# Decays by a tree of pairs, and another order of the groups of an RWKV-7 attention kernel with hash-routed experts

## The chip, the cores and the metric

The kernel runs on one core of one Trainium2 chip. Its time is the device time of the execution in microseconds (us); lower is better. A core has five engines that run side by side, each through its own list of instructions in order: TensorE (PE, matrix products and transposes into PSUM), VectorE (DVE), ScalarE (ACT), GpSimd (POOL) and SyncE (SP, which here only issues DMA). In this kernel the order on PE, DVE, ACT and POOL is fixed by the program itself; SP's is chosen by the framework.

## The reference, cut to what matters

Two layers, one behind the other. The first is a recurrence over 768 steps for 4 batches x 8 heads with a 40 x 40 state:

```python
for t in range(S):                                     # S = 768, D = 40
    y[:, :, t] = einsum('bhd,bhde->bhe', r_t, state)
    Sa = einsum('bhde,bhe->bhd', state, a_t)
    state = state * w_t[:, :, None, :] - einsum('bhd,bhe->bhde', Sa, b_t) + einsum('bhd,bhe->bhde', v_t, k_t)
```

Its output, turned to 3072 rows of 320, goes to 8 experts, chosen by a hash of the token's id:

```python
expert_idx = token_ids * 2654435761 % 8
out[mask_e] = np.maximum(x[mask_e] @ w1[e], 0) @ w2[e]     # 320 -> 1024 -> 320
```

## The kernel before: the parts that matter

The recurrence is done in chunks of 64 steps. A *tile* is one chunk of two batches; there are 24 (tile `u`). Four tiles make a *group*, and two chunks of all batches make a *round of decays* (6 rounds; round `ri` serves tiles 4ri to 4ri+3). Within a chunk the products of `w` scale the other inputs: `pb` holds the reciprocals of such products, `qb` the products up to the chunk's end. Each group needs the inverse of triangular matrices, done by substitution on DVE.

Every piece of work is put down with a *tick*; the program sorts them by tick and writes them out in that order. Within a tick the position is given by a name:

```python
STEPS = ["r1", "r0", "z", "nc", "y", "at_t", "x", "x_t", "s", "u", "r_t", "sd", "a", "rc"]
LAG = 8          # tile u is recurred on (tile_b) at tick u + 8; its inputs are prepared (tile_a) at tick u
GRP = 4
```

The round of decays, in segments of 8 steps:

```python
def decays(ri, t_w, t0, span, t_f, span_f=None, stores=None):
    @at_tick(t_w)
    def _():
        x["qb"] = qb = early.tile([P, (HC + 1) * D], F32, tag="qb", name="qb", bufs=2)
        ...                                   # four DMAs load w into qb
        x["pb"] = early.tile([P, (HC + 1) * D], F32, tag="pb", name="pb", bufs=2)[:, 0:HC * D]
        nc.gpsimd.memset(segs(x["pb"])[:, :, 0, :], 1.0)

    for i in range(1, SL):                    # SL = 8: seven products of 128 x 160
            p = segs(x["pb"])
            nc.vector.tensor_tensor(p[:, :, i], p[:, :, i - 1], segs(x["qb"])[:, :, i - 1], op=OP.mult)
    for i in range(SL - 2, -1, -1):           # and seven more
            q = segs(x["qb"])
            nc.vector.tensor_tensor(q[:, :, i], q[:, :, i], q[:, :, i + 1], op=OP.mult)
    ...     # own: the products of the segments
    ...     # f_ps: PE brings the partner half's product; ends; rends = 1 / ends (128 x 160)
    ...     # half_p, half_q: pb * rends and qb * ends, two products of 128 x 640 each
    ...     # round 0: two transposes to p_rows, q_rows in SBUF; else: both are stored to DRAM
```

The preparation of a tile, and the inversion of a group:

```python
def tile_a(u):
    @at_tick(u - 1.7)      # loads: pl, ql (the decays, by GpSimd), al, kb (a, b, k, by SyncE); two buffers each
    ...
    @at_tick({0: -0.6, 1: -0.4, 2: 0.4, 3: 1.4}.get(u, u + late - (0.1 if late else 0.6)))
        ...                # DVE: at = -a * p ; z = kb * q
    @at_tick(u + late, "at_t")   # PE turns at, ACT copies
    @at_tick(u + late, "z")      # PE turns z, ACT copies
    @at_tick(u + late, "a")      # PE: the scores a_ps; ACT copies pk, no; DVE: mk

def group_i(gi, t0, t1, t2):
    ...     # DVE: nu <- pk (a transpose), 30 pairs outer = u * n, u += outer, then ut, ug (two transposes)
```

The recurrence of a tile, where PE's order is what the change touches:

```python
def tile_b(u, t0):
    @at_tick(t0 - 1, "r0")      # r1_ps  = at_t x sb     (sb: the state, copied by ACT at "rc" of tile u - 2)
    @at_tick(t0, "r1")          # r1_ps += mk x v        ; ACT copies r1
    @at_tick(t0, "nc")          # um x r1                ; ACT copies into x
    @at_tick(t0, "x_t")         # PE turns x             ; ACT copies
    @at_tick(t0, "s")           # s_ps = state + z x x   ; DVE: st = s_ps * decay
    @at_tick(t0, "rc")          # rc_ps = r_t x x_t      ; DVE: mr
    @at_tick(t0 + 1, "y")       # y = r_t x sd + mr x z  ; DVE: xs = y * p ; GpSimd stores xs
    @at_tick(t0 + 1, "sd")      # PE turns the state     ; ACT copies
    # tile_m: "x" and "u" at t0 - 1 use ut, ug of the group's inverse; tile_s: loads r, v at t0 - 2
```

And where it all stands:

```python
decays(0, -4.0, -3.0, 0.4, -2.5, 0.3)
decays(1, -2.9, -1.9, 0.4, (-0.55, ...), stores=1.34)
decays(2, -0.65, 0.87, 0.45, (1.87, 1.9, ...), stores=3.34)
for ri in range(3, NR):
    t0 = ri * RN * NG - 5.0                  # ri * 4 - 5
    decays(ri, t0 - 1.0, t0 + 0.25, 1.0, t0 + 1.3, 1.1)
for gi in range(NU // GRP):
    t0 = gi * GRP + GRP - 1 + t_a
    group_i(gi, t0 + 0.05, t0 + 0.1, t0 + 3.4)
# routing(): which token goes to which slot of which expert, in small steps on DVE
    t = 4.5 if i < 1 else NU + 3.35 + 0.105 * (i - 12) if i > 11 else 9.3 + 1.1 * i
```

The expert layer follows after the last tile: matrix products over eight experts, whose weights stream in.

Of the kernel before, what the change touches and what calls it, by code (L numbers as in the profile page):

```python
# [36 lines left out]
F32 = mybir.dt.float32  # L37
# [10 lines left out]
def kernel(  # L48
# [90 lines left out]
    def early_weights():  # L139
# [3 lines left out]
        w2s[0] = [early.tile([P, (C // 2 + 1) * D], F32, tag=n, name=f"w2_0{n}", bufs=2)[:, 0:FP // 2 * DM]  # L143
# [24 lines left out]
    STEPS = ["r1", "r0", "z", "nc", "y", "at_t", "x", "x_t", "s", "u", "r_t", "sd", "a", "rc"]  # L168
# [143 lines left out]
    SEG = 4  # L312
    HC = C // 2
    SL = HC // SEG

    def decays(ri, t_w, t0, span, t_f, span_f=None, stores=None):
# [4 lines left out]
        def segs(t):  # L321
            return t[:, 0:HC * D].rearrange("p (s t e) -> p s t e", s=SEG, e=D)
# [12 lines left out]
        @at_tick(t_w)  # L335
        def _():
            x["qb"] = qb = early.tile([P, (HC + 1) * D], F32, tag="qb", name="qb", bufs=2)

            dma = (nc.sync.dma_start, nc.scalar.dma_start if ri < 2 else nc.sync.dma_start)
            for y in range(2 * RN):  # L340
                src = w.rearrange("b h (n t) e -> (b h) n (t e)", t=HC)[:, ri * 2 * RN + y]
                dma[y % 2](qb[y * BH:(y + 1) * BH, 0:HC * D], src)
            x["pb"] = early.tile([P, (HC + 1) * D], F32, tag="pb", name="pb", bufs=2)[:, 0:HC * D]
            nc.gpsimd.memset(segs(x["pb"])[:, :, 0, :], 1.0)


        for i in range(1, SL):
            @todo.append
            def _(i=i):
                p = segs(x["pb"])  # L350
                nc.vector.tensor_tensor(p[:, :, i], p[:, :, i - 1], segs(x["qb"])[:, :, i - 1], op=OP.mult)
        for i in range(SL - 2, -1, -1):
            @todo.append
            def _(i=i):
                q = segs(x["qb"])
                nc.vector.tensor_tensor(q[:, :, i], q[:, :, i], q[:, :, i + 1], op=OP.mult)

        @todo.append
        def _():

            q = segs(x["qb"])
            x["own"] = own = work.tile([P, SEG, D], F32, tag="own", name="own", bufs=1)
            nc.vector.tensor_copy(own[:, SEG - 1], q[:, SEG - 1, 0])
            for s in range(SEG - 2, -1, -1):
                after_s = q[:, s + 1, 0] if s == SEG - 2 else own[:, s + 1]
                nc.vector.tensor_tensor(own[:, s], q[:, s, 0], after_s, op=OP.mult)  # L366

        def half_p(some):

            p = segs(x["pb"])[:, some]  # L370
            by = x["rends"][:, some].unsqueeze(2).to_broadcast([P, SEG // 2, SL, D])
            nc.vector.tensor_tensor(p, p, by, op=OP.mult)

        def half_q(some):
            q = segs(x["qb"])[:, some]
            by = x["ends"][:, 1:][:, some].unsqueeze(2).to_broadcast([P, SEG // 2, SL, D])
            nc.vector.tensor_tensor(q, q, by, op=OP.mult)

        @then.append
        def _():  # L380
            x["f_ps"] = p = bank([P, D], "f_ps")
            nc.tensor.matmul(p, lhsT=partner[:], rhs=x["own"][:, 0], start=True, stop=True)  # L382

        @then.append
        def _():

            x["ends"] = ends = work.tile([P, SEG + 1, D], F32, tag="ends", name="ends", bufs=1)
            nc.vector.tensor_scalar(ends[:, SEG], x.pop("f_ps"), second[:, 0:1], None, op0=OP.add)
            nc.vector.tensor_tensor(ends[:, 0:SEG], x["own"][:],
                                    ends[:, SEG].unsqueeze(1).to_broadcast([P, SEG, D]), op=OP.mult)  # L390

        @then.append
        def _():
            ends = x["ends"]
# [867 lines left out]
```

## Time and profile before

| | |
|---|---|
| time, median of 3 runs | 668.7 us (665.96 to 676.79) |
| the profiled execution, span | 663.8 us |
| PE, DVE, ACT, POOL busy | 562.9, 365.7, 296.7, 195.3 us |
| attention part, about | 0 to 411 us |
| expert layer, about | 411 to 664 us |
| DMA packets | 195,771, of which 176,718 under 512 B |
| moved | 85.14 MB |

The profile is of one execution. Its page gives the busy time of each engine, the span in 40 slices with tenths of busy time, the DMA queues, a chain of work that ended last, groups of instructions by line, and DMA issues. Answers of the trace give the same for any stretch: tables of stages, instructions in order of time with the idle time before each and who ended it, and lists of who waited for whom. "L479" is line 479 of the kernel; a line can be that of a helper that many operations share, so the names of the tiles tell more. Idle time of an engine that holds nobody up costs nothing.

### The profile page before, as it was taken

How to read it: one execution, taken by the hardware profiler on the slowest of the kernel's cores; microseconds unless marked ns; L12 is line 12 of the kernel's file. 1: busy time of each engine (PE TensorE's matmuls, PEld its weight loads, DVE VectorE, ACT ScalarE, POOL GpSimd, SP SyncE). 2: the span in 40 equal slices, each digit the busy share in tenths (PEclk: the TensorE clock that was granted, in tenths of full speed). 3: DMA queues.
4: the chain of work that ended last, by engine and by line, in shares of the span. 5: the costliest groups of instructions: out<-in, count | busy, mean ns of one | idle time of the engine just before them, and what ended most of it. 6: DMA issues, size and time to landing. Idle time of an engine off the chain costs nothing.

```text
span 663.8 us, 23022 instructions
## 1 busy us (share of the span) xinstructions
PE 562.9 (85%) x9866; PEld 428.9 (65%) x9866; DVE 365.7 (55%) x944; ACT 296.7 (45%) x695; POOL 195.3 (29%) x333
## 2 busy tenths in 40 slices
PE   0145558988988899899999988999999999999995
PEld 0134557777777788788888877775665656565653
DVE  6996977977886798689589843132030302023020
ACT  4043535765666687777767664112241313111010
POOL 0413331333333435334223321173314131212101
PEclk9976558998988999999999999999999999999999
DMA  7699996888488569774334541859243354121000
GB/s 133 175 169 177 162 168 114 157 156 152 104 158 157 117 129 185 125 142 96 62 81 83 126 127 34 267 183 318 89 152 90 129 199 161 48 100 40 30 12 24
DMA packets 195771, 85.14 MB, mean 128 GB/s; under 512 B 176718, under 2 KB 186191, under 8 KB 195664
## 3 DMA queue, kind: packets, MB, share of 16 engines
q1 hardware_dynamic: 184208, 46.25, 36.3%
q0 software_dynamic: 11264, 36.72, 19.7%
q8 instruction: 78, 1.28, 0.8%
q10 hardware_dynamic: 192, 0.66, 0.4%
q14 instruction: 29, 0.24, 0.1%
HBM read 66.54 MB, written 15.40 MB: 123 GB/s over the span
## 4 chain that ended last, share of the span: by engine, by line
PE 47%; issue 22%; DVE 14%; ACT 6%; DMA 5%; POOL 4%; SPq 1%; POOLq 0%; DVEq 0%; ACTq 0%
PE up_ps L1005 6%; PE dn_ps L1023 6%; PE y_ps L289 5%; PE s_ps L289 4%; PE x_t_ps L690 3%; PE a_ps L289 3%; PE t_ps L530 3%; PE r_ps L289 2%; POOL out_dram L1028 2%; PE z_ps L493 2%; PE x_ps L289 2%; PE nc_ps L289 2%; PE u_ps L289 2%; DVE outer L572 2%; PE sd_ps L750 2%
## 5 line engine op out<-in xcount | busy, mean ns | idle before, releaser
L1013 DVE TENSOR_SCALAR ht<-up_ps 128x416 f32<-128x416 f32 (+2 forms) x36 | 19.4, 543 | 166.1 <-PE up_ps L1010 164.7
L1023 PE MATMUL dn_ps<-w,ht 128*128 128x320 f32 x336 | 91.7, 433 | 0.0
L1005 PE MATMUL up_ps<-xt,w 128*128 128x416 f32 x224 | 81.3, 516 | 0.0
L1023 PEld LDWEIGHTS dn_ps<-w,ht 128*128 128x128 f32 x336 | 63.3, 190 | 25.5
L742 POOL DMA_DIRECT2D x_rows<-xs x44 | 23.2, 533 | 179.8 <-DVE xs L738 79.0
L1028 POOL DMA_INDIRECT out_dram<-o,idx_all x26 | 26.1, 1004 | 169.8 <-ACT o L1027 163.4
L572 DVE TENSOR_TENSOR outer<-nu 128x252 f32<-128x252 f32 (+8 forms) x180 | 63.4, 352 | 4.6
L579 DVE TENSOR_TENSOR nu<-nu,outer 128x252 f32<-128x252 f32 (+8 forms) x180 | 63.3, 352 | 4.5
L1005 PEld LDWEIGHTS up_ps<-xt,w 128*128 128x128 f32 x224 | 41.9, 190 | 36.8 <-issue 31.7
L1015 ACT ACTIVATE ht<-up_ps 128x416 f32<-128x416 f32 (+2 forms) x36 | 17.2, 479 | 107.5 <-PE up_ps L1010 107.4
L495 ACT COPY z_t<-z_ps 104x512 f32<-104x512 f32 x48 | 25.7, 588 | 66.0 <-PE z_ps L493 66.0
L1027 ACT COPY o<-dn_ps 128x320 f32<-128x320 f32 x26 | 11.1, 425 | 92.5 <-PE dn_ps L1023 92.5
L493 PE MATMUL z_ps<-ident,z 128*104 128x128 f32 x192 | 33.3, 331 | 15.2 <-DVE z L479 14.7
L460 POOL DMA_DIRECT2D pl<-p_rows x48 | 25.2, 531 | 51.7 <-DVE at L475 34.1
L289 PE MATMUL a_ps<-at_t,z_t 64*64 64x64 f32 x1536 | 32.0, 241 | 6.9 <-ACT at_t L531 6.9
L493 PEld LDWEIGHTS z_ps<-ident,z 128*104 128x104 f32 x192 | 26.0, 157 | 18.0 <-issue 15.5
L289 PEld LDWEIGHTS a_ps<-at_t,z_t 64*64 64x64 f32 x1536 | 28.4, 152 | 12.5 <-ACT at_t L531 9.5
L289 PE MATMUL rc_ps<-r_t,x_t 64*64 64x64 f32 x1536 | 29.9, 222 | 7.4 <-issue 6.7
L702 DVE TENSOR_TENSOR mr<-rc_ps,after 128x1024 f32<-128x1024 f32 x24 | 29.2, 1217 | 12.3 <-PE rc_ps L289 12.2
L523 DVE TENSOR_TENSOR mk<-a_ps,after 128x512 f32<-128x512 f32 x24 | 16.5, 688 | 30.5 <-ACT no L521 30.5
L289 PEld LDWEIGHTS rc_ps<-r_t,x_t 64*64 64x64 f32 x1536 | 25.8, 134 | 9.6 <-issue 8.5
L382 PE MATMUL f_ps<-own,partner 128*128 128x40 f32 x12 | 3.2, 359 | 33.6 <-DVE own L366 33.6
(227 smaller groups left out, 1168.6 us busy)
## 6 DMA issues: line engine op xcount, KB each, us to landing
ql<-q_rows POOLq DMA_DIRECT2D x48, 160.0 KB, 4.6
w<-in_moe_w_dram SPq DMA_DIRECT2D x10, 640.0 KB, 8.7
w<-in_moe_w_dram SPq DMA_DIRECT2D x10, 512.0 KB, 3.7
al<-in_a_dram SPq DMA_DIRECT2D x48, 80.0 KB, 4.6
kb<-in_b_dram SPq DMA_DIRECT2D x48, 80.0 KB, 4.1
kb<-in_k_dram SPq DMA_DIRECT2D x48, 80.0 KB, 4.1
pl<-p_rows POOLq DMA_DIRECT2D x48, 80.0 KB, 4.1
r<-in_r_dram SPq DMA_DIRECT2D x48, 80.0 KB, 3.9
```

Of the source, the lines that this page charges most:

```text
L289: nc.tensor.matmul(out_, lhsT=lhsT, rhs=rhs, start=start, stop=stop, skip_group_check=True)
L460: nc.gpsimd.dma_start(pl[half(be)], of_batches(p_rows, 2 * g + be, 1))
L493: nc.tensor.transpose(p[0:R, be, hp * P:(hp + 1) * P], x["z"][:, be, hp, :], ident[:])
L495: nc.scalar.copy(t[0:R, be].rearrange("p h t -> p (h t)"), p[0:R, be])
L530: nc.tensor.transpose(p[:, hp, :], src[:, hp, :], ident[:])
L572: nc.vector.tensor_tensor(tv, paired(x["u"])[:, 0:full[1], j:j + 1, :].to_broadcast(full), paired(x["n"])[:, j // 2, j + 1:, j % 2].unsque ...
L579: nc.vector.tensor_tensor(o, o, x["t"][:, 0:n].rearrange("p (c i k) -> p c i k", c=full[1], k=2), op=OP.add)
L702: nc.vector.tensor_tensor(t[:].rearrange("p two h t -> p (two h) t"), p[:].rearrange("p two (h t) -> p (two h) t", t=C), after[:].unsqueez ...
L742: dma(x_of[2 * g + be, n * C:(n + 1) * C], xs[half(be), :])
L1005: nc.tensor.matmul(p[:], lhsT=w1[c][:, (f0 + i) * P:(f0 + i + 1) * P], rhs=xt[:, c, 0:n], start=(c == 0), stop=False)
L1023: nc.tensor.matmul(p[i * m:(i + 1) * m], lhsT=ht[:, f, c0:c0 + m], rhs=w2[f // (FP // 2)][:, f % (FP // 2), :], start=(f == 0), stop=(f == ...
L1028: st = nc.gpsimd.indirect_dma_start(out=out[:], out_offset=bass.IndirectOffsetOnAxis(ap=idx, axis=0), in_=o[0:m], in_offset=None, bounds_c ...
```

## The change

Five things are changed together.

- **The tree.** A round of decays makes its running products by a tree of pairs: up through five levels of products of neighbours (widths 320, 160, 80, 40, 40 per side), then down again (40, 80, 160, 320, 640). It does the same with fewer elements. `w` is loaded into a tile of its own, `wt`, with one buffer, and is read until the end of the way down.
- **The order of PE's groups.** `STEPS` has another order, and `r0` of a tile stands at its own tick, ahead of `r1`, not a tick earlier.
- **The third round of decays** (`decays(2, ...)`) moves from ticks 0.87 to 2.2 behind the first inversion, to 7.2 to 8.1, and the fourth to 8.6 to 10.4.
- **The third group of tiles** (8 to 11) is prepared at ticks 10.4 to 11.75, close together, tiles 12 and 13 at 12.5 and 13.2; the group's inversion follows.
- **The routing's** first steps move from ticks 10.4 to 21.4 to 24.05 to 27.05, and one of its tiles shares memory with another.

The purpose is to let the first inversion, which the recurrence waits for, begin without the third round's work and stores in front of it, and to take work off DVE.

```diff
-    STEPS = ["r1", "r0", "z", "nc", "y", "at_t", "x", "x_t", "s", "u", "r_t", "sd", "a", "rc"]
+    STEPS = ["r0", "r1", "z", "y", "nc", "x", "at_t", "x_t", "s", "u", "sd", "a", "r_t", "rc"]
...
         @at_tick(t_w)
         def _():
-            x["qb"] = qb = early.tile([P, (HC + 1) * D], F32, tag="qb", name="qb", bufs=2)
+            x["w"] = wt = early.tile([P, HC * D], F32, tag="wt", name="wt")
...
+        for lv in range(1, LV + 1):
             @todo.append
-            def _(i=i):
-                p = segs(x["pb"])
-                nc.vector.tensor_tensor(p[:, :, i], p[:, :, i - 1], segs(x["qb"])[:, :, i - 1], op=OP.mult)
+            def _(lv=lv):
+                ...
+                i = nodes(lv - 1)
+                if lv == LV:
+                    x["own"] = own = work.tile([P, D], F32, tag="own", name="own", bufs=1)
+                    nc.vector.tensor_tensor(own[:].unsqueeze(1), i[0], i[1], op=OP.mult)
+                else:
+                    for j, o in enumerate(nodes(lv)):
+                        nc.vector.tensor_tensor(o, *(t.rearrange("p (k two) e -> p two k e", two=2)[:, j] for t in i), op=OP.mult)
+
+        def spread(t, first, levels):
+            for lv in levels:
+                size = 1 << lv
+                at = pairs(t, size)
+                i = nodes(lv)
+                if first:
+                    nc.vector.tensor_tensor(at[:, size], at[:, 0], i[0], op=OP.mult)
+                else:
+                    nc.vector.tensor_tensor(at[:, size - 1], at[:, 2 * size - 1], i[1], op=OP.mult)
...
+    LATE = {4: 4.45, 5: 5.3, 6: 6.15}
+    CLOSE = {8: 10.4, 9: 10.85, 10: 11.3, 11: 11.75}
+    AFTER = {12: 12.5, 13: 13.2}
...
-        @at_tick(u + late, "at_t")
+        @at_tick(ta + 0.43 if close else ta, None if close else "at_t")
...
-        @at_tick(t0 - 1, "r0")
+        @at_tick(t0, "r0")
...
-    decays(1, -2.9, -1.9, 0.4, (-0.55, -0.54, -0.53, -0.35, -0.34, -0.3, -0.29, 0.2), stores=1.34)
-    decays(2, -0.65, 0.87, 0.45, (1.87, 1.9, 1.91, 2.0, 2.01, 2.1, 2.11, 2.2), stores=3.34)
-    for ri in range(3, NR):
+    decays(1, -2.15, -1.9, 0.4, (-0.55, -0.54, -0.53, -0.35, -0.34, -0.3, -0.29, 0.2), stores=1.34)
+    decays(2, -0.25, 7.2, 0.3, 7.5, 0.6)
+    decays(3, 8.25, 8.6, 0.8, 9.4, 1.0)
+    for ri in range(4, NR):
         t0 = ri * RN * NG - 5.0
-        decays(ri, t0 - 1.0, t0 + 0.25, 1.0, t0 + 1.3, 1.1)
+        decays(ri, t0 - 0.6, t0 + 0.25, 1.0, t0 + 1.3, 1.1)
...
-        t0 = gi * GRP + GRP - 1 + t_a
-        group_i(gi, t0 + 0.05, t0 + 0.1, t0 + 3.4)
+        t0 = t_of(gi * GRP + GRP - 1) + t_a
+        group_i(gi, t0 + 0.05, t0 + 0.1, (gi + 2) * GRP - 0.81)
...
-        rst = route.tile([P, E, TPP], F32)
+        rst = route.tile([P, E, TPP], F32, name="rst", tag="sel")
...
-        t = 4.5 if i < 1 else NU + 3.35 + 0.105 * (i - 12) if i > 11 else 9.3 + 1.1 * i
+        t = 4.5 if i < 1 else NU + 3.35 + 0.105 * (i - 12) if i > 11 else NU - 0.25 + 0.3 * i
```

## The prediction

> **What bounds the kernel now.** I read the slices first, because they show where each engine has air.
>
> ```profile
> PE   0145558988988899899999988999999999999995
> ...
> DVE  6996977977886798689589843132030302023020
> ...
> PEclk9976558998988999999999999999999999999999
> DMA  7699996888488569774334541859243354121000
> ```
>
> One slice is 16.6 us. Up to slice 6 (100 us) TensorE is mostly idle while DVE and DMA are nearly full. Slices 7 to 17 have PE and DVE both high; to 20 PE alone; from 25 the expert layer, which the change leaves alone. So the stages have different limits, and I cut the attention part at the starts of the `x_ps` groups of tiles 0, 4, 8, 12, 16, 20 (94, 151, 217, 273, 325, 366 us). Each of those groups needs the inverse of its four tiles, and the table by stage (columns: us; busy us and count of PE, PEld, DVE, ACT, POOL; clock; DMA share; GB/s) says who sets them.
>
> ```profile
> 58.00:94.00 36.00, 18.30 (x256) 15.99 (x256) 30.37 (x77) 13.71 (x30) 10.68 (x22) 0.50 0.99 167
> 94.00:151.00 57.00, 48.35 (x1345) 41.74 (x1345) 47.04 (x118) 36.75 (x88) 17.83 (x35) 0.90 0.77 141
> 151.00:217.00 66.00, 55.49 (x1494) 48.34 (x1489) 50.41 (x129) 40.97 (x98) 22.18 (x44) 0.92 0.76 143
> 217.00:273.00 56.00, 50.36 (x1498) 43.65 (x1491) 48.83 (x133) 40.74 (x97) 21.67 (x42) 1.00 0.75 142
> 273.00:325.00 52.00, 49.07 (x1452) 42.81 (x1448) 40.26 (x102) 39.31 (x92) 19.77 (x38) 1.00 0.56 106
> 325.00:366.00 41.00, 40.05 (x1242) 35.09 (x1240) 32.13 (x81) 29.86 (x69) 13.61 (x26) 1.00 0.39 81
> ```
>
> From 58 to 94 the first inversion runs alone on DVE, with DMA at 0.99: start-up is a DVE chain behind loads. From 94 to 217 nobody is full (DVE 83% and 76%, PE 85% and 84%): they wait for each other. From 217 to 273 DVE is the limit (48.8 of 56), then PE (49.1 of 52, 40.1 of 41). Four late tiles cost 41 us against 52 because the tile-A work (`z`, `at_t`, `a`) has ended.
>
> How the start-up hangs together is in the timeline (start, length, operation, in brackets the idle time before it and its releaser), of PE and then of DVE:
>
> ```profile
> 44.99 0.65 PE L382 MATMUL f_ps<-own,partner 128*128 128x40 f32 x2 [4.64 <-DVE own L366]
> 45.44 1.93 PE L493 MATMUL z_ps<-ident,z 128*104 128x128 f32 x8
> ...
> 94.10 1.06 PE L289 MATMUL x_ps<-ut,no 32*32 32x32 f32 x32 [3.69 <-DVE ut L587]
> ```
>
> ```profile
> 37.81 0.83 DVE L479 TENSOR_TENSOR z<-kb,ql 128x640 f32<-128x640 f32 x1 [0.93 <-DMA kb<-in_k_dram]
> ...
> 58.43 1.23 DVE L554 STREAM_TRANSPOSE nu<-pk 128x1024 f32<-128x1024 f32 x1
> ...
> 86.67 0.82 DVE L479 TENSOR_TENSOR z<-kb,ql 128x640 f32<-128x640 f32 x1 [3.62 <-DMA kb<-in_k_dram]
> ```
>
> `z` of tile 2 was ready on DVE at 38.6, yet PE took it up at 45.4: ahead of it in PE's order stands `f_ps` of the third round of decays, whose `own` DVE made only at 44.9. That delays tile 3, so the first inversion starts at 58.4; a late `kb` costs it 3.6 us; its end releases `x_ps` at 94.1.
>
> [...]
>
> ```profile
> L356 DVE TENSOR_TENSOR qb<-qb 128x160 f32<-128x160 f32 x42 | 13.5, 321 | 1.0
> ...
> L372 DVE TENSOR_TENSOR pb<-pb,rends 128x640 f32<-128x640 f32 x12 | 9.6, 819 | 0.1
> ...
> L366 DVE TENSOR_TENSOR own<-qb,own 128x40 f32<-128x40 f32 x12 | 2.4, 200 | 0.4
> ...
> L396 DVE RECIPROCAL rends<-ends 128x160 f32<-128x160 f32 x6 | 6.9, 1147 | 0.1
> ```
>
> So halving the tree saves most while the tiles are wide. [...]
>
> **Part 1, the tree.** A round before: 14 products of 160 at 0.321 = 4.5, `own` 0.8, `ends` 0.6, reciprocal of 160 1.15, four products of 640 at 0.82 = 3.3, copy 0.2: 10.5 us. After: up 2 x (0.49+0.32+0.24+0.20)+0.20 = 2.7; `ends` 0.45; a reciprocal of 40, by width 1.15/4 = 0.3; down twice 0.20+0.24+0.32+0.49+0.82 = 4.1: 7.6 us. Saved about 3 us a round. But the tree reads `w` up to its last product, and `wt` has one buffer where `qb` had two: a load of `w` can start only when the round before has ended.
>
> **Part 2, start-up.** Round 0 ends with `q_rows` at about 21.8 (23.3 before). The load of round 1 starts at 19.2, when `wt` is free, and lands at 24 (4.6 us by the page's list of DMA issues): some 2 us of idle DVE, so `own` of round 1 comes at 27 for 28.9 and `z` of tile 1 at about 31 for 33.4. PE no longer meets `f_ps` of round 2, so `z` of tile 2 runs at about 37.5. But on sync's queue the load of round 2 now stands in the middle of tile 3's loads, and waits for the end of round 1 (35.4); `b` and `k` of tile 3 go out until about 40.5 and land near 45. There tile 3 was before (45.35), but then PE lost six us, taking it up at 51.4. Now it takes it at 46; with the 7.0 us from there to the transpose in before (51.41 to 58.43), the inversion starts at 53, 5.4 us earlier. Its length was 36.7, less the 3.6 of `kb` (two stores of 640 KB are gone from ahead of the loads), plus about 1.5 for tile 4, whose loads still stand behind the stores of round 1. `x_ps` of tile 0: 94.1 - 5.4 - 2.5 = about 86. **Gain 8.**
>
> **Part 3, tiles 0 to 4.** DVE from the end of the first inversion to that of the second: inversion 26.3 (60 products of 21.1 and 1.3 of gaps, transposes 3.7), rounds 2 and 3 at 7.8 each, 3 x (`mr` 1.2, `st` 0.6, `xs` 0.5) = 7, three `at`/`z` 3.6, two `mk` 1.2: 54, where before it had 47 and 8 of waiting. New waits: 2 for `a` of tile 7, 1 to 2 for `f_ps` and `s_ps`, and about 5 for `w` of round 3, whose load stands on sync behind round 2's stores and behind `wt`. Sum 62: `x_ps` of tile 4 at 149 for 150.4. **The gain shrinks to 1**, but a round of decays has been done more than before.
>
> **Part 4, tiles 4 to 12.** The next four: DVE 54 (inversion 26.3, one round, five `at`/`z`, six `mk`, four of the rest), PE 4 x 9.7 (the spacing of late tiles, 347.3 to 357.0) + 6 x 2.6 (`z` 1.0, `at_t` 0.6, `a` 1.0) = 54. Two equal engines, coupled: about 60, against 66. Then DVE 51 (no routing, cheaper round) and PE 49: 52.5, against 56. **Gain 11 at tile 12.**
>
> **Part 5, the order of PE.** `r0` moves behind the copy of the state it needed, and `y` goes ahead of `nc`. The waits of `r_ps` for `sb` are 4.4 us between 94 and 260, and after that:
>
> ```profile
> PE r_ps L289 <- ACT sb L724: 2.5, 4, 0.8
> ```
>
> In the DVE-bound stages this buys nothing; between tiles 12 and 16 I count 2. **Gain 13.**
>
> **Part 6, the routing.** Its first steps, 8.6 us of DVE by their rows, move from 139..301 us to ticks 24 to 27, where the last inversion runs beside tiles without A-work. DVE took 33.9 us there before (333.5 to 367.4) and PE waited for it by 0.33 us only. Adding 8.6 and 0.3 of gaps, less 1.7 of idle time, makes PE wait 7 us at tile 20. **Gain 6 at the end**; the expert layer follows as before.
>
> **Sum:** 8 - 7 + 10 + 2 - 7 = 6, so 668.7 - 6 = 662.7; I say 662.
>
> **Rivals.** (a) The start-up gain survives in full: the wait for `w` in part 3 is filled by other loads, and the idle PE between 94 and 217 (19 us) shrinks because rounds no longer sit in the same ticks as the loads. For it: DVE is 76% busy in 151..217, with no work missing. Then 668.7 - 14 = 650 to 655. (b) Loads become the bound between tiles 0 and 5: two rounds of stores and the loads of tiles 8 to 13 now fall in about 60 us, 16,384 + 18,432 packets of 160 B and `r`, `v` of 10,240; at 36.3% of 16 engines for 184,208 packets (1.3 ns each) that is 59 us. Against it: before ran at shares of 1.0 without more than 3.6 us lost at once. Then nothing is gained before tile 8, and the routing costs its 7: 670 to 675. (c) The routing is absorbed, because DVE, no longer late, begins the last inversion sooner: but its start hangs on `a` of tile 23, which PE sets. It would give 655.
>
> **Range and chances.** (a) and (c) pull to 650, (b) to 673; the three runs of before themselves span 666 to 677. Range 650 to 673. Faster by over 2% is under 655.3: it needs (a) or (c), 0.22. Slower by over 2% (over 682) needs (b) and a new wait at each tick: 0.03. Within: 0.75.
>
> **What would show it.** Round of decays near 7.6 us; PE at `z` of tile 2 before 40 us; first inversion from about 53, `x_ps` of tile 0 near 86, of tile 4 near 149; a DVE wait of some 5 us for `wt` before the fourth round; no wait of `r_ps` for `sb`; PE waiting about 7 us for `ut` at tile 20. I am wrong if tile 0 comes after 92, if PE does not wait at tile 20, or if the stretch between tiles 4 and 12 is not shorter than 122 us.

## The result, and the profile after

The changed kernel takes **675.5 us** (median of 4 runs, 673.6 to 675.8) against 668.3 for the kernel before: ratio 1.011, 95% interval [1.008, 1.015]. It is slower, and above the predicted range (650 to 673). The profiled execution spans 671.8 us, that of before 663.8.

The starts of `x_ps`, at which the prediction cut the kernel, say where (us; "predicted" is worked out from the prediction's own stretches):

| | tile 0 | 4 | 8 | 12 | 16 | 20 | end |
|---|---|---|---|---|---|---|---|
| before | 94.1 | 150.4 | 216.5 | 272.4 | 325.1 | 366.4 | 663.8 |
| predicted | 86 | 149 | 209 | 261.5 | 312 | 360 | 657.8 |
| after | 85.3 | 148.1 | 217.6 | 270.5 | 322.4 | 371.8 | 671.8 |

Up to tile 4 the prediction holds within 1 us. From tile 4 to 8 it took 69.5 us where 60 was predicted and 66.1 was measured before. Tiles 4 to 12 together took 122.4 us, and not less than 122 was a mark of being wrong that the prediction had named. Tiles 16 to 20 cost 8.1 more than before (7 predicted), and 2.7 more are lost behind tile 20, where nothing was expected.

The same slices as shown of before (here 16.8 us each):

```profile
PE   0363682997889998999997998999999999999995
...
DVE  6738975884599798687689751331130302023020
...
PEclk9985567798989999999989798999999999999998
DMA  5999849299698779773333351669352455131000
```

In slices 5 to 7 (84 to 134 us) DMA reads 4, 9, 2, where before it read 9, 6, 8; then 9, 9. PE has a hole in slice 6 (a 2), DVE is low in slices 6, 9 and 10 (5, 4, 5). The table by stage, cut as before:

```profile
51.40:85.30 33.90, 16.19 (x238) 14.04 (x240) 29.96 (x76) 12.82 (x28) 10.56 (x21) 0.50 0.93 157
85.30:148.10 62.80, 46.11 (x1170) 39.91 (x1170) 47.43 (x128) 30.34 (x76) 18.70 (x36) 0.79 0.65 122
148.10:217.60 69.50, 59.21 (x1635) 51.67 (x1631) 47.15 (x119) 46.39 (x111) 24.95 (x48) 0.93 0.86 164
217.60:270.50 52.90, 50.38 (x1483) 43.66 (x1483) 45.27 (x115) 39.92 (x96) 21.90 (x42) 1.00 0.80 153
270.50:322.40 51.90, 49.56 (x1490) 43.24 (x1482) 38.83 (x93) 39.30 (x92) 19.84 (x38) 1.00 0.57 114
322.40:371.80 49.40, 42.43 (x1252) 36.90 (x1248) 39.86 (x119) 30.52 (x72) 13.65 (x26) 0.96 0.33 68
```

From tile 0 to 4 (second row) PE did 46.1 us of work in 62.8, with 175 matrix products fewer than before in that stretch; the third row has 141 more than before (1635 for 1494), and 59.2 us of PE. Work was moved from a stretch where PE stood idle for 16.7 us into one where it is busiest. DMA moved the same way: 0.65, then 0.86, for 0.77 and 0.76 before.

The start-up on PE (start, length, operation, in brackets the idle time before it and its releaser):

```profile
39.99 1.95 PE L498 MATMUL z_ps<-ident,z 128*104 128x128 f32 x8 [1.32 <-DVE mk L528]
...
85.26 1.06 PE L289 MATMUL x_ps<-ut,no 32*32 32x32 f32 x32 [2.82 <-DVE ut L592]
...
116.03 1.93 PE L289 MATMUL y_ps<-z,mr 128*64 128x40 f32 x32 [12.02 <-DVE mr L707]
```

`z` of tile 2 is on PE at 40.0 (45.4 before), the first inversion starts at 51.4 (58.4), `x_ps` of tile 0 at 85.3. Then PE stands for 12 us at 116.0 for `mr`. DVE's timeline has the start of the first inversion, what stood ahead of `mr`, and what came later:

```profile
51.42 1.24 DVE L559 STREAM_TRANSPOSE nu<-pk 128x1024 f32<-128x1024 f32 x1
...
110.87 0.49 DVE L366 TENSOR_TENSOR pb<-wt 128x320 f32<-128x320 f32 x1 [7.56 <-DMA wt<-in_w_dram]
...
134.81 0.82 DVE L377 TENSOR_TENSOR qb<-qb,wt 128x640 f32<-128x640 f32 x1
...
159.43 0.49 DVE L366 TENSOR_TENSOR pb<-wt 128x320 f32<-128x320 f32 x1 [10.42 <-DMA wt<-in_w_dram]
...
178.01 1.19 DVE L559 STREAM_TRANSPOSE nu<-pk 128x1024 f32<-128x1024 f32 x1
```

DVE waited for `w` 7.6 us ahead of the fourth round and 10.4 us ahead of the fifth. The second wait has its origin on sync's queue (start and length of the issues):

```profile
132.17 1.27 SPq L308 DMA_DIRECT2D al<-in_a_dram  x2
...
136.86 4.26 SPq L337 DMA_DIRECT2D p_rows<-pb  x3
141.22 2.75 SPq L308 DMA_DIRECT2D al<-in_a_dram  x2
144.06 2.23 SPq L308 DMA_DIRECT2D kb<-in_b_dram  x2
146.34 1.31 SPq L308 DMA_DIRECT2D kb<-in_k_dram  x2
147.70 4.88 SPq L337 DMA_DIRECT2D q_rows<-qb  x4
152.63 2.48 SPq L352 DMA_DIRECT2D wt<-in_w_dram  x4
```

`qb` of the fourth round was finished at 135.6, its store went out at 147.7, and the load of `w` behind it landed at 159.4. From 132.2 on the queue issued almost without a break: the loads of tile 10, three stores of `p_rows`, the loads of tile 11, and only then the store of `q_rows`. Only a small part of this is a wait: `al` of tile 10 was held for 1.9 us, until `at` of tile 8, which reads the same buffer, had ended at 132.1, and nothing else went out on the queue from 130.2 to 132.2. The rest, from 132.2 to 147.7, is the time that the issues take (15.05 us by their lengths).

The inversion for tiles 8 to 11, which begins with the transpose `nu<-pk`, started at 178.0. `z` of tile 11, which stands right behind the second wait in DVE's order, was made at 160.6; PE made the scores `a` of tile 11 from it at 173.2, and DVE stood 4.1 us for `y_ps` and 4.4 us for `no`, which is copied from these scores. In the kernel before:

```profile
159.39 1.24 DVE L554 STREAM_TRANSPOSE nu<-pk 128x1024 f32<-128x1024 f32 x1
```

18.6 us sooner, 9 us behind `x_ps` of tile 4 instead of 30.

The tree's products cost what was worked out, 0.23 to 0.24 us at 80 wide, 0.48 to 0.49 at 320 and 0.82 at 640; only the reciprocal of 40 took 0.40 for 0.3. (The kernel before has 0.48 for `xs`, 320 wide; a straight line between its 0.200 at 40 wide and its 0.321 at 160 gives 0.24 at 80, an estimate.)

### The profile page after: what moved, and what is told of

Its sections match the earlier page's. It is cut to its first block, busy times and chain, and to the rows that moved or that the text cites. A ratio compares the mean times of both kernels' runs of the same rounds, so it can differ in the third digit from the quotient of the medians.

```text
span 671.8 us, 22958 instructions
## 1 busy us (share of the span) xinstructions
PE 568.0 (85%) x9866; PEld 433.9 (65%) x9866; DVE 349.8 (52%) x920; ACT 295.2 (44%) x695; POOL 194.6 (29%) x327
## 4 chain that ended last, share of the span: by engine, by line
PE 39%; issue 21%; DVE 18%; SPq 8%; DMA 6%; POOL 4%; ACT 2%; POOLq 0%; DVEq 0%; ACTq 0%
PE up_ps L1011 6%; PE dn_ps L1029 6%; SPq L308 4%; PE y_ps L289 4%; PE s_ps L289 3%; DVE outer L577 3%; DVE nu L584 3%; SPq L337 3%; PE x_t_ps L695 3%; POOL out_dram L1034 2%; PE rc_ps L289 2%; DVE mr L707 2%; PE a_ps L289 2%; PE r_ps L289 2%; PE nc_ps L289 2%
## 5 line engine op out<-in xcount | busy, mean ns | idle before, releaser
L584 DVE TENSOR_TENSOR nu<-nu,outer 128x252 f32<-128x252 f32 (+8 forms) x180 | 63.5, 353 | 4.6
L498 PE MATMUL z_ps<-ident,z 128*104 128x128 f32 x192 | 33.0, 328 | 20.5 <-DVE z L484 15.6
L289 PE MATMUL y_ps<-z,mr 128*64 128x40 f32 x768 | 27.8, 232 | 23.8 <-DVE mr L707 23.3
L467 POOL DMA_DIRECT2D pl<-p_rows x48 | 25.3, 532 | 68.4 <-DVE at L480 26.5
L685 ACT COPY x<-nc_ps 64x320 f32<-64x320 f32 x48 | 20.2, 420 | 53.4 <-PE nc_ps L289 52.8
L289 PEld LDWEIGHTS y_ps<-z,mr 128*64 128x64 f32 x768 | 25.6, 141 | 25.7 <-DVE mr L707 25.2
L289 PE MATMUL a_ps<-at_t,z_t 64*64 64x64 f32 x1536 | 33.4, 244 | 8.6 <-ACT at_t L536 6.4
```

Of the source, the lines that this page charges most:

```text
L289: nc.tensor.matmul(out_, lhsT=lhsT, rhs=rhs, start=start, stop=stop, skip_group_check=True)
L467: nc.gpsimd.dma_start(pl[half(be)], of_batches(p_rows, 2 * g + be, 1))
L498: nc.tensor.transpose(p[0:R, be, hp * P:(hp + 1) * P], x["z"][:, be, hp, :], ident[:])
L584: nc.vector.tensor_tensor(o, o, x["t"][:, 0:n].rearrange("p (c i k) -> p c i k", c=full[1], k=2), op=OP.add)
```

## The experiments

All times are medians; the ratio is to the kernel before, run beside. Compare kernels by ratio, because the times of before moved between 666.7 and 668.3 in the median. The starts of `x_ps` come from one execution each: the changed kernel, e2 and e3 have the same work up to tile 0 and reach it at 85.3, 86.8 and 87.1, so differences of 2 us between the stretches of two kernels say little. One slip first: in the expectations of e1, e2 and e4 "tile 8 (190.6)" is the start of `x_ps` of tile 6; tile 8 comes at 217.6. The expected stretches are read below with the right tile.

| run | what | us | ratio, interval | tile 0 | 4 | 8 | 12 | 16 | 20 |
|---|---|---|---|---|---|---|---|---|---|
| e1 | changed, two buffers for `w` | 669.9 | 1.006 [1.003, 1.008] | 83.4 | 138.7 | 210.6 | 263.5 | 315.7 | 365.2 |
| e2 | changed, loads of tiles 10, 11 later | 679.4 | 1.022 [1.017, 1.027] | 86.8 | 149.7 | 218.1 | 276.9 | 327.4 | 378.4 |
| e3 | changed, routing back | 675.8 | 1.012 [1.009, 1.016] | 87.1 | 149.9 | 223.2 | 279.7 | 330.5 | 372.2 |
| e4 | changed, serial rounds | 680.9 | 1.023 [1.020, 1.026] | 84.6 | 145.8 | 221.0 | 275.0 | 327.4 | 377.4 |
| e5 | e1 less 12 loads | 655.5 | 0.984 [0.978, 0.990] | 82.8 | 137.6 | 201.1 | 255.4 | 308.1 | 359.5 |
| e6 | before + tree | 655.1 | 0.985 [0.978, 0.991] | 92.4 | 146.6 | 206.7 | 262.2 | 316.1 | 357.4 |
| e7 | before + tree + order | 653.6 | 0.982 [0.976, 0.988] | 96.6 | 151.8 | 205.7 | 262.1 | 314.1 | 355.5 |
| e8 | before + order | 660.9 | 0.991 [0.987, 0.994] | 97.1 | 152.3 | 210.6 | 267.6 | 321.9 | 363.4 |
| e9 | changed, third round and group back | 658.6 | 0.982 [0.974, 0.990] | 91.3 | 145.8 | 201.6 | 259.1 | 311.9 | 362.4 |
| e10 | e8, clean start | 662.4 | 0.989 [0.985, 0.993] | 94.9 | 151.6 | 209.1 | 267.9 | 320.9 | 362.4 |
| e11 | e7, clean start | 652.5 | 0.975 [0.968, 0.982] | 93.1 | 149.1 | 206.0 | 260.9 | 312.9 | 354.4 |
| e12 | e11, third round beside the inversion | 652.2 | 0.975 [0.969, 0.981] | 92.2 | 146.2 | 200.9 | 258.6 | 312.0 | 353.4 |
| e13 | e9, routing back | **646.5** | **0.969** [0.962, 0.977] | 90.7 | 143.1 | 198.1 | 257.0 | 308.5 | 350.0 |
| e14 | e1, third group sooner | 659.5 | 0.988 [0.985, 0.991] | 82.4 | 142.9 | 207.3 | 260.7 | 315.0 | 365.2 |

### First theory: the single buffer of w (e1, e2)

The theory after the trace: the two waits for `w` are the loss. e1 takes them away.

```diff
-            x["w"] = wt = early.tile([P, HC * D], F32, tag="wt", name="wt")
+            x["w"] = wt = early.tile([P, HC * D], F32, tag="wt", name="wt", bufs=2)
-                        x[n] = early.tile([P, HC * D], F32, tag=n, name=n, bufs=2)
+                        x[n] = early.tile([P, HC * D], F32, tag=n, name=n, bufs=1 if n == "pb" else 2)
-    decays(3, 8.25, 8.6, 0.8, 9.4, 1.0)
+    decays(3, 6.6, 8.6, 0.8, 9.4, 1.0)
-        decays(ri, t0 - 0.6, t0 + 0.25, 1.0, t0 + 1.3, 1.1)
+        decays(ri, t0 - 2.0, t0 + 0.25, 1.0, t0 + 1.3, 1.1)
```

> The changed kernel with two buffers for w (and one for pb, so that it fits; the first expert's and the routing's small tiles take the second w buffer), and the loads of w of rounds 3 to 5 asked for 1.4 to 1.65 ticks sooner. Theory (the single buffer costs the gain: VectorE stands in order for w, 7.6 us before the fourth round and 10.4 before the fifth): both waits fall under 1.5 us, x_ps of tile 4 comes at about 142 (148.1 in the changed kernel), of tile 8 at about 176 (190.6), and the time is 656 to 664 (675.5). Rival (the loads are the bound between tiles 0 and 8): the wait moves to the tiles' own loads (al, kb), tile 8 stays after 186, and the time is 670 to 676.

Both waits are gone. Tile 4 comes 9.4 us sooner, so the wait ahead of the fourth round was a real loss. But from tile 4 to 8 it takes 71.9 us, longer than before, and the time falls by 5.6 us only (3.9 by the ratios): the theory is half right, the rival right on the mechanism, while its numbers (tile 6 after 186, 670 us or more) are missed just, by 183.9 and 669.9. The wait went to the tiles' loads. e1's DVE, then its PE:

```profile
152.47 0.49 DVE L480 SCALAR_TENSOR_TENSOR at<-al,pl 128x320 f32<-128x320 f32 x1 [3.40 <-DMA al<-in_a_dram]
157.37 0.82 DVE L484 TENSOR_TENSOR z<-kb,ql 128x640 f32<-128x640 f32 x1 [4.41 <-DMA kb<-in_k_dram]
```

```profile
159.39 1.95 PE L498 MATMUL z_ps<-ident,z 128*104 128x128 f32 x8 [7.51 <-DVE mr L707]
```

DVE stands 3.4 and 4.4 us for `al` and `kb` of tile 12; behind that in its order is `mr`, for which PE stands 7.5 us; behind that on PE are `z` and `a` of tile 11; and the third inversion starts at 171.4, 33 us behind `x_ps` of tile 4. From 145 to 165 us the DMA share was 1.02 and 0.99 there.

e2 tests the place in the queue alone.

```diff
-        @at_tick(ta - 1.7)
+        @at_tick(ta - (1.35 if u in (10, 11) else 1.7))      # loads of tiles 10 and 11
```

> The changed kernel, where only the loads of tiles 10 and 11 are asked for 0.35 ticks later, so that on sync's queue the store of q_rows of the fourth round and the load of w of the fifth stand ahead of the loads of tile 11. Theory (the 10.4 us for w come from the place in the queue: q was ready at 135.6 and its store went out at 147.7): the store goes out by 138, w lands by 150, the wait falls under 3 us, tile 8 comes at 181 to 184 (190.6), and the time is 665 to 670 (675.5). Rival (VectorE's wait is not what sets tile 8; the matrix engine or tile 11's late loads are): tile 8 within 2 us of 190.6, time within 3 us of 675.5.

The store of `q_rows` went out at 140.7 (147.7), the wait ahead of the fifth round fell from 10.4 to 4.0 us, so the queue was its cause. Yet the third inversion started at 177.3 (178.0) and the stretch took 68.4 us: DVE now waited for tile 11's `al`, `kb` and for `ql`. The rival holds on what it says of the stretch (tile 6 at 191.0 for 190.6): this wait only hid another. The edit pays for the shorter wait with later loads of tile 11, so it shows what sets the wait, and not that a wait costs nothing. The time rose by 4 (7 by the ratios), for which the trace has 5.9 us between tiles 8 and 12, at a mean clock of 0.94 for 1.00, and no cause in the edit that I can name.

### The loads, the rounds, the routing (e3, e4, e5)

e5 starts from e1 and leaves work out: tiles 10 and 11 compute with `a`, `b`, `k` of tiles 8 and 9.

```diff
-            x["kb"] = kb = work.tile([P, 2, DM], F32, tag="kb", name="kb")      # and the same for al
+            x["kb"] = kb = tiles[u - 2]["kb"] if u in (10, 11) else work.tile([P, 2, DM], F32, tag="kb", name="kb")
+            if u in (10, 11): return                                            # no loads of a, b, k
```

> The kernel of e1_two_w, but tiles 10 and 11 take a, b and k of tiles 8 and 9 from the buffers where they already lie: twelve loads of 80 KB are left out, and no instruction of the engines. Theory (between tiles 4 and 8 the loads are the bound: DMA share 1.02 and 0.99 from 145 to 165 us, VectorE then 35% busy): VectorE's waits for al and kb between 140 and 158 (13 us) fall under 3, from tile 4 (138.7) to tile 8 (210.6) it takes 58 to 63 instead of 72, and the time is 656 to 662 (669.9). Rival (the order of the groups puts tile 11 late, loads or no loads, and the third inversion with it): still over 68, time 667 or more.

The waits for `al` and `kb` are gone, the third inversion starts at 162.1 instead of 171.4, the stretch falls from 71.9 to 63.5 us. The loads are thus the cause of some 8 us of it. (Of the 9.5 us won at tile 8, 5.7 are left at tile 20; the rest of the 12.5 us between the two profiled executions lies behind it, where e1 ran at half clock for 10 us, see the last section.) The stretch does not fall to the 55.8 of e9 below: of the 63.5, PE is busy for 56.4.

e4 puts back the serial rounds with their two buffers (`decays` as in the kernel before, at the changed ticks).

> The changed kernel with the round of decays of before (chains in four segments, 10.5 us each, two buffers into which w is loaded), all else as changed. Theory (the tree saves 3 us a round but its one buffer gives it back): no wait for w over 2 us in rounds 3 and 4; tile 0 at 87 to 90 (85.3), tile 4 at 148 to 152 (148.1), tile 8 at 184 to 188 (190.6), time 668 to 675 (675.5). Rival (the tree is worth its 3 us in each of six rounds, and the waits for w are only where VectorE would wait for something else): tile 8 after 193, time 680 to 690.

The expected wait did not vanish: DVE stood 15.5 us for `w` ahead of the fifth round, *with* two buffers, because the load was asked for late and stood behind the same stores. Slower by 5 us than the changed kernel (8 by the ratios). The rival's two numbers hold, just (tile 6 at 193.9, 680.9 us), though 5 to 8 us are less than 3 in each of six rounds. The tree is a gain in the changed kernel too, and a second buffer alone does not remove the wait.

e3 puts the routing's first steps back:

```diff
-        t = ... else NU - 0.25 + 0.3 * i
+        t = ... else 9.3 + 1.1 * i
```

> The changed kernel with the first twelve routing steps back where they were (from tick 9.3, 1.1 apart). Theory: from tile 16 to 20 takes 42 us (49.4), the matrix engine does not wait for ut before tile 20; 8.6 us of VectorE's work come back between tiles 4 and 16, of which 4 to 6 show from tile 8 to 12, where VectorE is the bound; the time is 670 to 674 (675.5). Rival 1 (VectorE has room between tiles 4 and 16, as it stands waiting there): nothing is given back, 666 to 668. Rival 2 (the stretch from tile 16 to 20 is long for the lower clock and the new order, not for the routing): it stays over 47, and the time does not fall.

From tile 16 to 20 it takes 41.8 us (49.4), as the theory has it, but 7.4 of these 7.6 us come back between tiles 4 and 12 (129.8 us for 122.4). In the changed kernel the move of the routing cost nothing.

### Each part alone (e6 to e11)

e6 is the kernel before with the tree (two buffers for `w`, one for `pb`), all ticks of before.

> The kernel before with the tree alone, with two buffers for w (and one for pb, so that it fits) and every tick of before. Theory (the tree is worth what its rounds save, where VectorE is the bound: in the start-up, and from tile 8 to 12): tile 0 at 89 to 92 (94.1 before), from tile 8 to 12 it takes 53 to 54 (55.8), time 660 to 664 (667 to 668 before). Rival 1 (the 3 us are hidden, as VectorE waits elsewhere): within 2 us of before. Rival 2 (the tree's products in the stream of the inversion, or the lost second buffer of pb, cost more than they save): slower than before.

Faster by 1.5%, more than expected: tile 0 is 1.7 us sooner, from 4 to 8 it takes 60.2 us (66.1). The third round waited 7.1 us for the store of `p_rows` out of the single `pb`.

e7 adds the order, e8 has the order alone:

```diff
-    STEPS = ["r1", "r0", "z", "nc", "y", "at_t", "x", "x_t", "s", "u", "r_t", "sd", "a", "rc"]
+    STEPS = ["r0", "r1", "z", "y", "nc", "x", "at_t", "x_t", "s", "u", "sd", "a", "r_t", "rc"]
-        @at_tick(t0 - 1, "r0")
+        @at_tick(t0, "r0")
```

> The kernel of e6_tree_alone with the new order of the matrix engine's groups as well. Theory (part 5 of the prediction): r_ps no longer waits for sb, which shows by 0 to 3 us, most of it from tile 12 to 16 and in the last tiles: 0 to 3 us below e6_tree_alone. Rival (the new order makes y_ps wait for mr, up to 23 us in sum in the changed kernel, which is a loss of its own): 3 us or more above e6_tree_alone.

> The kernel before with the new order of the matrix engine's groups alone. Theory: 0 to 3 us faster than before (667 to 668). Rival (y_ps, now ahead of nc, comes before mr is made, and holds the queue): 3 us or more slower than before.

In these two, `at_t` of tile 0 comes at tick 0.43, behind the 0.4 at which `at` of tile 2 is written into the same buffer: tiles 0 and 1 took `at` of tiles 2 and 3, and waited for it. That is what the change's 0.4 to 0.45 is for. e10 and e11 have it.

```diff
-        @at_tick({0: -0.6, 1: -0.4, 2: 0.4, 3: 1.4}.get(...
+        @at_tick({0: -0.6, 1: -0.4, 2: 0.45, 3: 1.45}.get(...
```

> As e8_order_alone, with at and z of tiles 2 and 3 made 0.05 ticks later, as in the changed kernel: in e8_order_alone (and e7_tree_order) at of tile 2 went into the buffer that tile 0 had not yet been read from, so that tiles 0 and 1 took at of tiles 2 and 3, and waited for it. Theory: the first x_ps comes at 93 to 95 instead of 97.1, from tile 4 to 8 it takes 58 to 60, as in e8_order_alone, and the time is 656 to 659 (660.9). Rival (the late start and the short stretch belong together: what was late at tile 0 is only caught up): tile 4 at 150, and from tile 4 to 8 it takes 62 or more; 661 to 665.

> As e7_tree_order (tree with two buffers for w, new order, all ticks of before), with the same 0.05 ticks. Theory: tile 0 at 91 to 93, as in e6_tree_alone (92.4), for 96.6, and of those 4 us at least 2 stay: 649 to 652 (653.6). Rival: the start is caught up by tile 8 anyway, within 1 us of e7_tree_order.

The order alone is worth 1.1%, some 7 us (e10; its start came 2.2 us sooner and the time did not fall against e8, within the intervals). From tile 4 to 8 it takes 57.5 us instead of 66.1; 3 us of that are lost from 8 to 12. The rival, that `y` held up PE, is out. Tree and order together: 2.5% (e11). There tile 0 comes 3.5 us sooner than in e7, and the two are level at tile 8. The median falls by 1.1 us, by the ratios it is 5, and the intervals overlap: what is left of the sooner start is open.

e9 undoes in the changed kernel the shift alone: third round, third group, and with them the ticks of the loads of `w` and of the inversions' ends, all as before. One buffer for `w`, and the late routing, stay.

```diff
-    CLOSE = {8: 10.4, 9: 10.85, 10: 11.3, 11: 11.75}
-    AFTER = {12: 12.5, 13: 13.2}
-    decays(1, -2.15, -1.9, ...)
-    decays(2, -0.25, 7.2, 0.3, 7.5, 0.6)
-    decays(3, 8.25, 8.6, 0.8, 9.4, 1.0)
-    for ri in range(4, NR):
+    decays(1, -2.9, -1.9, ...)
+    decays(2, -0.65, 0.87, 0.45, (1.87, ..., 2.2), stores=3.34)
+    for ri in range(3, NR):
-        decays(ri, t0 - 0.6, t0 + 0.25, 1.0, t0 + 1.3, 1.1)
+        decays(ri, t0 - 1.0, t0 + 0.25, 1.0, t0 + 1.3, 1.1)
```

> The changed kernel with only the third round of decays and the third group of tiles put back to their ticks of before (and with them the loads of w and the ends of the inversions); tree, one buffer for w, new order and late routing stay. Theory (the shift behind the first inversion is the loss: it bunches the loads of tiles 8 to 13 with two rounds of stores into 95..115 and 135..170 us): tile 0 comes later than the 85.3 of the changed kernel, at 90 to 95, but from tile 4 to 8 it takes 54 to 60 (69.5), and the time is 655 to 661 (675.5). Rival (the one buffer for w is the loss wherever the rounds stand): waits for w of 7 us and more stay before the fourth and the fifth round, and the time is 667 or more.

The decisive run: 658.6 us, within the theory. Tile 0 is 6 us later than in the changed kernel, and the stretch from tile 4 to 8 takes 55.8 us instead of 69.5. With one buffer, DVE does not wait for `w` ahead of the fourth and fifth rounds at all; 2.7 and 2.0 us ahead of the second and third is all that is left. The stretch from tile 4 to 8 of e1, e5, e9, in this order, in the columns of the table by stage:

```profile
138.70:210.60 71.90, 57.00 (x1635) 49.85 (x1631) 47.34 (x119) 46.69 (x113) 24.96 (x48) 0.93 0.85 159
```

```profile
137.60:201.10 63.50, 56.38 (x1641) 49.23 (x1633) 48.06 (x119) 46.39 (x111) 24.89 (x48) 0.97 0.83 160
```

```profile
145.80:201.60 55.80, 50.45 (x1490) 43.59 (x1483) 44.17 (x114) 39.93 (x96) 21.84 (x42) 1.00 0.77 151
```

e9 has 145 matrix products and 6.6 us of PE's work fewer there than e1: they were done before tile 4, beside the second inversion. The third inversion, at 154.1, starts 8 us behind tile 4 (30 in the changed kernel):

```profile
154.08 1.24 DVE L553 STREAM_TRANSPOSE nu<-pk 128x1024 f32<-128x1024 f32 x1
```

Nor is the loss only moved: up to tile 8 the changed kernel and e9 have done the same work (3346 and 3345 matrix products, 399 operations of DVE each), and e9 is there 16 us sooner. Half of that is idle time of PE (8.3 us), half a slower PE (busy 138.7 and 130.9 us, at clocks of 0.83 and 0.88).

### What is left of the start-up's gain, and the routing (e12 to e14)

e12 moves the third round only a little:

```diff
-    decays(2, -0.65, 0.87, 0.45, (1.87, 1.9, 1.91, 2.0, 2.01, 2.1, 2.11, 2.2), stores=3.34)
+    decays(2, -0.65, 1.5, 0.4, (3.2, 3.22, 3.3, 3.4, 3.5, 3.6, 3.7, 3.75), stores=4.0)
```

> The kernel of e11_tree_order_clean with the third round of decays moved by a little only: its tree behind z of tile 3, its product with partner behind z of tile 3 on the matrix engine, its end ahead of the first inversion, its stores at tick 4.0. Theory (the start-up's gain does not need the third group behind the first inversion, only z of tiles 2 and 3 ahead of the third round): the first inversion starts by 55 (59.7 in e6_tree_alone), tile 0 at 85 to 89, time 644 to 649. Rival (the stores, later, hold up the loads of tiles 4 to 8, and it is given back): tile 4 at 146 to 152 as in e6 and e7, and within 2 us of e11_tree_order_clean.

The inversion began at 56.1 instead of 61.2, but ended 0.9 us sooner only, and the time is the same: the rival.

e13 is e9 with the routing back (the diff of e3).

> The kernel of e9_group_back with the first twelve routing steps back at their ticks of before as well. Theory (the routing's 8.6 us of VectorE cost 8 to 9 us wherever the engines are the bound, which between tiles 4 and 16 they are once the third group stands where it stood): from tile 16 to 20 it takes 41 to 42 (50.4), 4 to 8 us are given back between tiles 4 and 16, time 654 to 659 (658.6). Rival (in the middle there is room for them, only the late place costs): nothing given back, 649 to 652.

The rival holds, and the time is under its range: **646.5 us**, 3.1% under the kernel before and the best of all. From tile 16 to 20 it takes 41.5 us (50.5), and from tile 4 to 16 165.4 (166.1): nothing is given back. The two stretches, e9 and e13:

```profile
311.90:362.40 50.50, 43.84 (x1258) 38.21 (x1252) 39.71 (x119) 30.73 (x72) 13.62 (x26) 0.93 0.33 66
```

```profile
308.50:350.00 41.50, 39.71 (x1254) 35.03 (x1247) 32.64 (x82) 29.45 (x70) 13.62 (x26) 1.00 0.40 80
```

DVE has 7 us less to do there, PE idles 1.8 us instead of 6.7, and its clock is 1.00 for 0.93.

e14 keeps the third group behind the inversion, but sooner:

```diff
-    CLOSE = {8: 10.4, 9: 10.85, 10: 11.3, 11: 11.75}
-    decays(3, 6.6, 8.6, 0.8, 9.4, 1.0)
+    CLOSE = {8: 9.7, 9: 10.2, 10: 10.7, 11: 11.3}
+    decays(3, 6.6, 8.9, 0.8, 9.75, 1.0)
```

> The kernel of e1_two_w (third group behind the first inversion) with its tiles 8 to 11 at ticks 9.7, 10.2, 10.7, 11.3 instead of 10.4, 10.85, 11.3, 11.75 and the fourth round 0.3 ticks later, so that the loads of tiles 10 and 11 stand on sync's queue ahead of the stores of the fourth round. Theory (between tiles 4 and 8 the path is: buffers of tiles 8 and 9 free, loads of tiles 10 and 11, their a, third inversion): the third inversion starts by 162 (171.4 in e1_two_w), from tile 4 to 8 it takes 60 to 65 (72.0), time 656 to 662 (669.9). Rival (VectorE and the matrix engine have the same work to do in any order, and what is won here is lost from tile 0 to 4): tile 8 after 207, time 666 or more.

With all work kept and the loads of tiles 10 and 11 ahead of the stores, the third inversion starts at 161.3 and the stretch takes 64.4 us instead of 71.9: the theory's chain, helped by some tile work that now comes before tile 4 (1565 matrix products in the stretch instead of 1635). But from tile 0 to 4 it takes 60.5 instead of 55.3, so 3.3 of the 7.5 us are left at tile 8 (207.3, just over the rival's 207), and none at tile 20. The time falls by 10 us, into the theory's range, but in the profiled executions, which differ by 6.6 us, all of that lies behind tile 20, where e1 ran at half clock for 10 us (last section). So the chain is as the theory has it, and its worth here stays open between 0 and 10 us; the kernel stays behind e9 and e13.

## Why the prediction was wrong

A ladder by the ratios, at 668 us: tree and order without the rest -3.1% (e13), -20.5 us; the late routing on top +8.4 (e9, -1.8%); the shift of the third round and group on top +19.7 (changed kernel, +1.1%). Sum +7.6. The change holds two gains and two losses, and the prediction had the signs of three. The steps of a ladder depend on their order: the shift on top of e13 is e3, which costs 29 us, and the late routing on top of that costs nothing. The shifts of the round and of the group were put back only together, so how the loss divides between them is open.

**Part 1, tree.** Right: 7.7 us a round by the measured lengths, 7.6 predicted. Alone it is worth 10 us (e6). The fear of the one buffer was right for the fourth round (7.6 us for the 5 predicted); the longer wait ahead of the fifth (10.4) was not foreseen. Neither is a property of the tree: both are gone at the old ticks (e9).

**Part 2, start-up.** Right within 2.5 us at each step: `z` of tile 2 at 40.0 for 37.5 (DVE waited 3.1 us for its `kb`), inversion at 51.4 for 53, tile 0 at 85.3 for 86. (The last step takes off 2.5 us where its own terms, 3.6 less 1.5, make 2.1.)

**Part 3, tiles 0 to 4.** Right in the sum, 62.8 for 63, and partly by luck: DVE was busy 47.4 us where the sum has 54, and it waited 13.1 us where the sum has 8 to 9. The 54 add up the lengths of the records, and neighbours among these overlap by up to 0.1 us: in the changed kernel the lengths in this stretch add up to 53 as well.

**Part 4, tiles 4 to 12.** The step that failed is its first half: "Two equal engines, coupled: about 60". It took the work of DVE (54) and PE (54) and added 6 of idle time. Measured: 69.5, with PE busy 59.2 and idle 10.3; of the 14 us by which the end was missed, 9.5 are here. PE's work was counted rightly (the scores `a` of six tiles lie in the stretch, 384 products of 64 a tile), but its mean clock was 0.93: (1 - 0.93) x 69.5 makes 5 us more, an estimate. The clock of the kernel before was 0.92 in that stretch, so there it is not the change's doing; the sum left it out. The idle time is no coupling of two full engines, as DVE was busy 47.2 only. It is a chain that the sum leaves out: buffers of tiles 8 and 9 free late, loads of tiles 10 and 11 with stores and `w` in one queue, `z` and `a` of tile 11, third inversion at 178.0. e5 (less loads: -8.4), e14 (tile 11 sooner: -7.5) and e9 (shift undone) show it; in e9 PE is idle 5.3 us in the stretch, at a clock of 1.00. The second half came out, 52.9 for 52.5, but not as put: it has DVE at 51 and PE at 49, and they were busy 45.3 and 50.4. In the kernel before, too, the prediction names DVE as the limit from 217 to 273 us (48.8), where its own table has PE at 50.4.

**Part 5, order.** What it names happened: `r_ps` waited 6.8 us for `sb` in the kernel before, and with the new order it does not (e10, changed kernel). The size is wrong ("In the DVE-bound stages this buys nothing; between tiles 12 and 16 I count 2"): about 7 us (e10), most of it between tiles 4 and 8. That it comes from these waits is not shown: only 1.2 us of them lie in that stretch. PE's idle time marked "issue" is 7.3 us there before and 3.3 in e10, and PE is busy 55.6 us at a clock of 0.92 before, 52.4 at 0.97 in e10. Why the order changes that is open. No run has the changed kernel with the old order, so what the order is worth in it is not known.

**Part 6, routing.** 8.1 for 7 at tile 20. The form was off: PE hardly waits for `ut` (0.6 us) but for `mr`, 5.5 us in four pieces, which stands behind the inversion and the routing in DVE's order; a clock of 0.96 over the 49.4 us makes another 2, an estimate. e3 shows that in the changed kernel the middle gains 7.4 us by the move, e13 shows none with the third group in its old place. Why the middle has room in the one and not in the other is argued from DVE's idle time, not shown.

**The end** was predicted to follow as before, and lost 2.7 us. Nearly all of it lies in the 50 us behind tile 20; the changed kernel and the one before:

```profile
371.81:413.00 41.19, 39.57 (x1068) 34.71 (x1070) 20.58 (x46) 26.06 (x60) 12.56 (x22) 0.89 0.43 110
413.00:671.80 258.80, 247.44 (x1248) 155.19 (x1244) 50.99 (x153) 48.70 (x99) 62.16 (x70) 0.99 0.37 119
```

```profile
366.45:405.00 38.55, 35.36 (x1039) 30.78 (x1043) 20.20 (x45) 25.34 (x59) 12.73 (x22) 1.00 0.50 118
405.00:663.80 258.80, 247.88 (x1269) 155.54 (x1260) 51.31 (x153) 48.99 (x100) 61.97 (x70) 1.00 0.36 119
```

Much the same work (1068 and 1039 matrix products in the records), at a clock of 0.89 instead of 1.00. The first `up_ps`, with which the expert layer begins, starts at 423.1 and 415.5, and from it to the end the two take 248.7 and 248.3 us. The prediction counted PE's waits and not the lower clock measured behind them here (0.50 from 372 to 376). It is no fixed price of the late routing: e5, e9 and e14 have it too, ran at half clock before tile 20 (last section), and took 295.2 to 295.5 us behind it, less than the kernel before (297.4).

**The rivals.** (b) came nearest: loads as the bound, 670 to 675. It placed them before tile 5, where the start-up's gain would have gone; they came between 4 and 8, with the gain still there. It was set against by "before ran at shares of 1.0 without more than 3.6 us lost at once", which says what loads cost in a schedule that spreads them, and nothing of one that bunches them. (a) is out, and (c) as it was put (tiles 16 to 20 take 8.1 us longer), though in the changed kernel the late routing costs nothing in the end (e3).

## What to carry to other kernels

When a change moves work later, don't add up each engine's work in a stretch: follow the chain that feeds the next bound step (buffer free, load issued, load landed, prepared, inverted) and ask at what time its first link can start. A wait with a name on it may hide another of the same length: DVE stood 10 us for `w`, and taking 6 of them away (e2) made the stretch 1 us shorter. Lengths of records are not busy time: 53 us of lengths were 47.4 busy. A change of several parts is worth taking apart even when the whole is a loss; here two of its parts alone make a kernel that is 3.1% faster than before.

## What was not expected of the hardware

A wait of PE was followed by half the clock. e9 at the place where the late routing makes PE wait for `mr` (steps of 2 us, columns of the table by stage):

```profile
345.00:347.00 2.00, 0.00 (x0) 0.00 (x0) 1.97 (x5) 0.00 (x0) 0.00 (x0) 1.00 0.00 0
347.00:349.00 2.00, 1.50 (x32) 1.50 (x32) 1.90 (x6) 0.00 (x0) 0.00 (x0) 0.69 0.03 8
349.00:351.00 2.00, 2.00 (x68) 1.85 (x66) 1.90 (x9) 0.59 (x2) 0.00 (x0) 0.50 0.00 0
```

PE stands for 3.9 us, and then runs at half clock until about 355: summed over the steps, (1 - clock) x 2 us gives another 3.4 us, an estimate. This is not one kernel's chance: all seven kernels with the late routing (changed, e1, e2, e4, e5, e9, e14) have such a stretch between 320 and 410 us; of the nine without it, before among them, only e10 has one (0.69 and 0.50 in the steps from 398 to 402). In five of the seven, e2, e4, e5, e9 and e14, PE stands once for 3.7 to 3.9 us (for `mr` in e9 and e14), and half clock begins between some 1.7 us ahead of the end of that wait (e2) and 1.4 us behind it (e5), an estimate from the means of the steps. In the other two no wait was as long: the changed kernel fell to 0.50 at 347 behind a wait of 0.9 us and at 371 behind 1.8 and 0.6, and e1 fell for 10 us at 388 behind pieces of 0.45 us marked "issue". A wait of 2.4 us was followed by half clock in e1 (at 354) and not in the changed kernel (at 358). What lowers the clock is not shown. These traces give no length of wait that decides.

And two buffers for `w` with one for `pb` (e11, 0.975) look worse than the reverse (e13, 0.969), though the intervals overlap: e11 waits 7.0 us in start-up for the store out of `pb`, e13 2.8 and 2.3 us for `w` ahead of the second and third rounds, and tile 0 comes at 93.1 and 90.7.
